# Cross attention and a GELU feed-forward block on one Trainium2 core: batch 1's second product in Strassen form, weight sums on GpSimd, another order of loads and outputs

## The chip, the cores and the metric

The kernel runs on one core of one Trainium2 chip. The metric is the device time of one execution in microseconds. The time before is the median of 8 runs. Beside it there is one profiled execution, whose span runs from its first to its last instruction.

## The reference

Eight batches of eight heads hold 512 rows of x and 32 rows of state, each of 64 columns. Attention goes both ways: every row of x reads the state, and every row of the state reads x. The results stand one below the other (512 + 32 = 544 rows for each batch), the heads side by side (512 columns). These 4352 rows then go through two matrix products with an exact GELU between them.

```python
scores  = scale * x @ state.T          # per batch and head
xread   = softmax(scores)  @ state     # 512 x 64
sread   = softmax(scale * state @ x.T) @ x   # 32 x 64
t = concatenate([xread, sread], rows)  # heads side by side: 4352 x 512
out = gelu(t @ w_in) @ w_out           # w_in 512 x 2048, w_out 2048 x 512
```

Inputs and outputs are float32; the products run on bfloat16 operands.

## The kernel before

The order of the work is written out by hand: a manual schedule, in which every engine executes its instructions in the order of the program text. The 512 rows of x of a batch are worked off batch by batch, and the 32 state rows of all eight batches are collected and go through the two products together at the end.

**Names of the steps.** For batch b:

- `load_x(b)` loads x into one of two buffers (xb) over the GpSimd queue. `rearr` and `rearr_ones` copy it into two layouts (x4, xo), two copies each on GpSimd from batch 2 on. `xtr_dma` transposes x4 by a DMA from SyncE's queue into xT; batch 1 is transposed on TensorE (`xtr`).
- `scores(b, half)` makes the scores on TensorE and their exponentials on ScalarE (e). `norm(b, half)` makes the row sums (cs, L344), their inverses (ics) and the product a = e * ics (L347) on VectorE. `atr` transposes a on TensorE, `atr_dma` by a DMA, into AT.
- `sread` and `sread_out` make the state rows' read-out (srm); `srt(b)` transposes it on TensorE and copies it on VectorE into XSR (L405).
- The first product is reassociated: P = state @ w_in, per head, in four chunks of 512 columns. `p_mm` computes one chunk in two PSUM tiles, `p_copy` copies the first on ScalarE (L426) and the second on VectorE (L427). `pmat` is one chunk; `burst` and `p_run` are several, all products ahead of all copies.
- `M(m, ...)` is `mm1`: the hidden units 128 m to 128 m + 127 of the rows of x, two matmuls of 512 columns and a GELU on ScalarE into g (L485). m counts on over the batches, 16 for each: M(16) is batch 1's first, M(32) batch 2's.
- `U(u)` is `mm2`: a quarter of the sum for one of four output tiles of a batch (j = 0..3), four matmuls of 512 columns (L504). u counts 16 for each batch. `mm2_m(b, m)` is one hidden block m for all four output tiles. With the last quarter VectorE copies the output tile out of PSUM (osb, L491), and SyncE's queue sends it.
- From batch 2 on, the second product is in Strassen form, with h over two halves of the rows, k over two halves of the hidden units and n over two halves of the output columns. `X(b, name)` is one of seven products, 16 matmuls of 256 columns (L602). `g_sum` makes its left operand on VectorE (gsum, L596); its right one is a quarter of w_out or one of five sums of quarters, made once by `w_sums(0)` to `w_sums(4)`, which are called 3, 4, 6, 1 and 7 (L570). The seven results are combined by copies on ScalarE (L640, L648, L652), sums on VectorE (L645, L656, L624, L658) and two instructions on GpSimd (L650, L621).
- `mm1_sr(m)` and `mm2_sr(s)` do the same two products for the state rows (L519, L531), with an output copy (L539) and transfer (L540).

**Order.** Loads stand on the GpSimd queue: w_in and w_out in pieces, then st (state), x(2) and x(3). `load_rest` issues those that are not needed at once. After a prologue for batch 0, the text mixes the steps of batches 0 and 1 by hand up to a first loop (p = 2 to 7), which ends batch 1's M and begins its U. A second loop runs over b = 2 to 7 with eight slots p: each slot has a pair M(16 b + 2 p, + 1) and, for b above 2, one X of the batch before, and in the last two slots X 3 and X 6 of its own. For b = 2 the remaining U of batch 1 stand in that place. In the last batch the slots p = 4 to 7 also take four `mm1_sr` each.

**PSUM.** `ftile` rotates through four banks (ps_f) for most small products. `otile` gives one of four other banks, by turn or by number: 3, 0, 1, 2 for batch 0's four output tiles, j = 0 to 3, and for `p_run(b, (0, 1), ((0, 1), (3, 2)))` banks 0, 1, 3 and 2.

Where POOL, PE, DVE, ACT and SP stand below, these are the profile's names of GpSimd, TensorE, VectorE, ScalarE and SyncE.

Of the kernel before, what the change touches and what calls it, by code (L numbers as in the profile page):

```python
# [10 lines left out]
BF16 = mybir.dt.bfloat16  # L11
# [6 lines left out]
def kernel(  # L18
# [8 lines left out]
    nc = tc.nc  # L27
# [4 lines left out]
    SB = S + NS  # L32
# [34 lines left out]
    w_out_bf = persist.tile([128, MC, d_model], BF16, name="w_out_bf")  # L67
    ident = persist.tile([128, 128], BF16, name="ident")
    sbd = persist.tile([128, B, HC, 2 * NS], BF16, name="sbd")
    XSR = persist.tile([128, HC, B * NS], BF16, name="XSR")  # L70
    g_sr = persist.tile([128, MC, B * NS], BF16, name="g_sr")
    st_f = persist.tile([128, 2, D], FP32, name="st_f")
    st_bf = persist.tile([128, B, 2, D], BF16, name="st_bf")
# [29 lines left out]
    def load_w_in(f0, f1):  # L103
        for t in range(2):
            nc.gpsimd.dma_start(  # L105
                out=w_in_bf[64 * t:64 * t + 64, :, f0:f1],
                in_=moe_w_in[256 * t:256 * t + 256, f0:f1].rearrange("(c d) f -> d c f", c=HC),
            )
# [3 lines left out]
    def load_w_out(i):  # L112
        nc.gpsimd.dma_start(out=w_out_bf[:, 4 * i:4 * i + 4, :], in_=w_out_r[:, 4 * i:4 * i + 4, :])

    def load_x(b):
        xb = xin.tile([128, H, SJ * D], BF16, name="xb", tag="xb")
        nc.gpsimd.dma_start(out=xb, in_=xr[b])
        xbs[b] = xb
# [12 lines left out]


    def load_rest():
        load_w_out(1)
        for f in range(2, FC):
            load_w_in(512 * f, 512 * f + 512)
            load_w_out(f)
        load_st(2, B)
        load_x(2)
        load_x(3)  # L140


# [221 lines left out]
    def atr_dma(b):  # L364
        A = atts[b]
        A.AT = att.tile([128, SJ, 2, 128], BF16, name="AT", tag="AT")
        nc.sync.dma_start_transpose(
            out=A.AT.rearrange("p j t n -> p (j t) n"), in_=A.a
        )
# [29 lines left out]
    def srt(b):  # L399
        A = atts[b]  # L400
        ps = ps_f.tile([128, HC, NS], BF16, name="srT", tag="f")
        nc.tensor.transpose(
            ps.rearrange("p c n -> p (c n)"), A.srm.rearrange("q t d -> q (t d)"), ident
        )
        nc.vector.tensor_copy(out=XSR[:, :, b * NS:(b + 1) * NS], in_=ps)  # L405

    Ps = {}

    def p_mm(b, f, tiles):
        if b not in Ps:  # L410
            Ps[b] = att.tile([128, 2, d_ff], BF16, name="P", tag="P")
        ps = [tiles([128, 512], "p_ps") for t in range(2)]
        for c in range(HC):
            for t in range(2):
                nc.tensor.matmul(  # L415
                    ps[t][32 * c:32 * c + 32, :],
                    lhsT=sbd[64 * t:64 * t + 64, b, c, 32 * t:32 * t + 32],
                    rhs=w_in_bf[64 * t:64 * t + 64, c, f * 512:(f + 1) * 512],
                    start=True,
                    stop=True,  # L420
                )
        return ps

    def p_copy(b, f, ps):
        dst = Ps[b][:, :, f * 512:(f + 1) * 512]
        nc.scalar.copy(out=dst[:, 0, :], in_=ps[0])  # L426
        nc.vector.tensor_copy(out=dst[:, 1, :], in_=ps[1])  # L427

    def pmat(b, f):
        p_copy(b, f, p_mm(b, f, ftile))  # L430

# [82 lines left out]
    def mm1_sr(m):  # L516
        hp = ps_f.tile([128, B * NS], FP32, name="hps", tag="f")
        for c in range(HC):
            nc.tensor.matmul(  # L519
                hp,  # L520
                lhsT=w_in_bf[:, c, m * 128:(m + 1) * 128],
                rhs=XSR[:, c, :],
                start=(c == 0),
                stop=(c == HC - 1),
            )
        nc.scalar.activation(out=g_sr[:, m, :], in_=hp, func=AF.Gelu)

    def mm2_sr(s):
        ps = ps_f.tile([128, d_model], FP32, name="ops", tag="f")
        for m in range(MC):  # L530
            nc.tensor.matmul(  # L531
                ps,
                lhsT=g_sr[:, m, s * 128:(s + 1) * 128],
                rhs=w_out_bf[:, m, :],
                start=(m == 0),
                stop=(m == MC - 1),
            )
        osb = opool.tile([128, d_model], FP32, name="osb", tag="osb")
        nc.vector.tensor_copy(out=osb, in_=ps)  # L539
        nc.sync.dma_start(  # L540
            out=out.rearrange("(b s) n -> b s n", s=SB)[4 * s:4 * s + 4, S:SB, :], in_=osb
        )


    def mm2_m(b, m):
        for j in range(SJ):
            if m == 0:
                ops[b, j] = otile([128, d_model], "op")
            nc.tensor.matmul(  # L549
                ops[b, j],  # L550
                lhsT=gs[b][:, m, j * 128:(j + 1) * 128],
                rhs=w_out_bf[:, m, :],
                start=(m == 0),
                stop=(m == MC - 1),
            )
# [5 lines left out]
    w_sum = {}  # L561

    def w_add(name, x, y, op):
        if name == "3":
            pair = persist.tile([128, 2, MH, NH], BF16, name="ws_34", tag="mix0")
            w_sum["3"], w_sum["4"] = pair[:, 0], pair[:, 1]
        elif name != "4":
            tag = {"6": "mix1", "1": "mix2", "7": "mix3"}[name]
            w_sum[name] = persist.tile([128, MH, NH], BF16, name=f"ws_{name}", tag=tag)
        nc.vector.tensor_tensor(out=w_sum[name], in0=x, in1=y, op=op)  # L570

    def w_sums(i):
        (b11, b12), (b21, b22) = w_q
# [120 lines left out]
    def M(*ms):  # L694
        for m in ms:
            mm1(m // MC, m % MC)

    def U(*us):
        for u in us:
            mm2(u // 16, u % 16 // 4, u % 4)  # L700
# [69 lines left out]
    scores(1, 0)  # L770
    scores(1, 1)
    srt(0)
    U(4, 5)
    rearr_ones(1)
    U(6)
    pmat(0, 2)
    norm(1, 0)
    norm(1, 1)
    U(7)
# [1 line left out]
    sread(1)  # L781
    sread_out(1)
    M(10, 11)
    mm2_m(0, 8)
    mm2_m(0, 9)
    burst([(0, 3), (1, 0)])
    mm2_m(0, 10)
    atr(1)
    M(12, 13)
    srt(1)  # L790
    M(14, 15)
    mm2_m(0, 11)
    begin(2)
    rearr(2)
    xtr_dma(2)
    rearr_ones(2)
    U(12)
    burst([(1, 1), (1, 2)])
    U(13)
    state_prep(2, B)  # L800
    M(16, 17)
    U(14)
    M(18, 19)
    U(15)
    burst([(1, 3), (2, 0), (2, 1)])
    U(16)


    u = 17
    for p in range(2, 8):  # L810
        if p == 4:
            scores(2, 0)
            scores(2, 1)
            norm(2, 0)
            norm(2, 1)
        if p == 7:
            atr_dma(2)
        if p == 3:
            begin(3)
            rearr(3)  # L820
            xtr_dma(3)
            rearr_ones(3)
        M(16 + 2 * p, 17 + 2 * p)
        U(u)
        u += 1
        if p in (5, 7):
            pmat(2, 2 + p // 7)
        if p >= 3:
            w_sums(p - 3)
        if p == 2:  # L830
            nc.gpsimd.tensor_copy(out=hold, in_=gs[1][:, 4, 0:1])
            load_x(4)

    for b in range(2, B):
        nb = b + 1
        for p in range(8):
            k = 16 * b + 2 * p
            if p == 1 and nb < B:
                scores(nb, 0)
                scores(nb, 1)  # L840
            if p in (2, 3) and nb < B:
                norm(nb, p - 2)
            if p == 3 and nb + 1 < B:
                xtr_dma(nb + 1)
            if p == 5 and nb < B:
                atr_dma(nb)
            M(k, k + 1)
            if nb == B and p >= 4:
                for m in range(4 * p - 16, 4 * p - 12):
                    mm1_sr(m)  # L850
            if b == 2:
                for _ in range(2 if p < 4 else 1):
                    if u < 32:
                        U(u)
                        u += 1
            elif p < 5:
                if p == 0:
                    g_sum(b - 1, "5")
                X(b - 1, "45127"[p])
                if p < 3:  # L860
                    g_sum(b - 1, "127"[p])
            if p == 1:
                sread(b)
                sread_out(b)
            if p == 0 and b + 3 < B:
                nc.gpsimd.tensor_copy(out=hold, in_=gs[b][:, 0, 0:1])
                load_x(b + 3)
            if p == 0 and nb + 1 < B:
                begin(nb + 1)
                rearr(nb + 1)  # L870
            if p == 2 and nb + 1 < B:
                rearr_ones(nb + 1)
            if p == 3:
                srt(b)
            if p == 5:
                g_sum(b, "6")
                if nb < B:
                    p_run(nb, (0, 1), ((0, 1), (3, 2)))
            if p == 6:
                X(b, "3")  # L880
            if p == 7:
                if nb < B:
                    p_run(nb, (2, 3), ((1, 2), None))
                X(b, "6")
# [46 lines left out]
```

## Time and profile before

| | us |
|---|---|
| median of 8 runs | 216.72 (215.59 to 218.07) |
| the profiled execution | 217.85 |
| its span | 216.1 |
| PE busy | 202.7 (94%) |
| PEld (weight loads) busy | 129.8 (60%) |
| DVE busy | 128.5 (59%) |
| ACT busy | 131.4 (61%) |
| POOL busy | 65.1 (30%) |

Busy times are unions over the instructions of an engine. PE and PEld are two rows of the same engine, matmuls and weight loads. Matmuls are pipelined, and the length of one in the profile (379 ns for 512 columns) holds its latency; what a stream of them takes is read from the chain of waits, where four take 0.86 us. The chain follows the work that ended last back to its beginning. In the rows of groups the columns are: line, engine, operation, output<-inputs, shapes, count | busy us, mean ns of one | idle us before, and what ended it. A granted clock of 1.00 is TensorE's full speed.

### The profile page before, as it was taken

How to read it: one execution, taken by the hardware profiler on the slowest of the kernel's cores; microseconds unless marked ns; L12 is line 12 of the kernel's file. 1: busy time of each engine (PE TensorE's matmuls, PEld its weight loads, DVE VectorE, ACT ScalarE, POOL GpSimd, SP SyncE). 2: the span in 40 equal slices, each digit the busy share in tenths (PEclk: the TensorE clock that was granted, in tenths of full speed). 3: DMA queues.
4: the chain of work that ended last, by engine and by line, in shares of the span. 5: the costliest groups of instructions: out<-in, count | busy, mean ns of one | idle time of the engine just before them, and what ended most of it. 6: DMA issues, size and time to landing. Idle time of an engine off the chain costs nothing.

```text
span 216.1 us, 4598 instructions
## 1 busy us (share of the span) xinstructions
PE 202.7 (94%) x1929; PEld 129.8 (60%) x1939; DVE 128.5 (59%) x206; ACT 131.4 (61%) x237; POOL 65.1 (30%) x71
## 2 busy tenths in 40 slices
PE   8889999998999999999999999999999969999960
PEld 7535444443444677667765777677667747886740
DVE  2934474739648559965996587558755512026340
ACT  3854865679875877587758775877584534650200
POOL 8954303481360055305571056002200220000400
PEclk9999999999999999999999999999999987999995
DMA  6999999789177619091909500700070010200332
GB/s 204 166 176 204 206 193 177 186 156 175 23 100 177 162 16 176 7 246 13 174 11 293 50 3 2 243 3 2 23 223 3 0 68 34 95 0 3 94 115 85
DMA packets 37837, 23.14 MB, mean 107 GB/s; under 512 B 21688, under 2 KB 35256, under 8 KB 37816
## 3 DMA queue, kind: packets, MB, share of 16 engines
q0 software_dynamic: 13936, 8.10, 27.7%
q1 hardware_dynamic: 23192, 14.29, 27.3%
q10 hardware_dynamic: 688, 0.46, 0.7%
q8 instruction: 15, 0.25, 0.4%
q14 instruction: 6, 0.05, 0.1%
HBM read 17.30 MB, written 8.91 MB: 121 GB/s over the span
## 4 chain that ended last, share of the span: by engine, by line
PE 82%; DMA 6%; POOL 5%; ACT 3%; issue 1%; DVE 0%; POOLq 0%; ACTq 0%
PE xp L602 34%; PE hp L478 24%; PE op L504 9%; DMA w_out_bf<-in_moe_w_out_dram 6%; PE p_ps L415 4%; PE hps L519 4%; PE ops L531 3%; POOL w_in_bf L105 2%; PE op L549 2%; PE pt L324 1%; PE sr L378 1%; POOL sbd L95 1%; ACT g L485 1%; ACT L485 1%; ACT L331 1%
## 5 line engine op out<-in xcount | busy, mean ns | idle before, releaser
L485 ACT ACTIVATE g<-hp 128x512 bf16<-128x512 f32 x124 | 67.5, 603 | 32.5 <-PE hp L478 27.6
L478 PE MATMUL hp<-AT,P 128*128 128x512 bf16 x248 | 63.9, 380 | 0.1
L602 PEld LDWEIGHTS <-gsum 128*128 128x128 bf16 x480 | 46.8, 98 | 12.1 <-issue 2.1
L596 DVE TENSOR_TENSOR gsum<-g 128x2048 bf16<-128x2048 bf16 x30 | 39.8, 1342 | 7.9 <-ACT g L485 6.8
L602 PE MATMUL xp<-ws,gsum 128*128 128x256 bf16 x288 | 34.8, 274 | 0.0
L478 PEld LDWEIGHTS <-P 128*128 128x128 bf16 x248 | 22.3, 98 | 20.4 <-issue 2.9
L427 DVE CAST P<-p_ps 128x512 bf16<-128x512 f32 x31 | 20.0, 684 | 18.5 <-PE p_ps L415 18.5
L650 POOL TENSOR_TENSOR u<-s,oh 128x512 f32<-128x512 f32 x6 | 8.0, 1331 | 71.6 <-ACT oh L648 71.6
L504 PE MATMUL op<-w_out_bf,g 128*128 128x512 bf16 x90 | 23.0, 379 | 0.4 <-DMA w_out_bf<-in_moe_w_out_dram 0.2
L602 PE MATMUL xp<-w_out_bf,gsum 128*128 128x256 bf16 x192 | 22.9, 273 | 0.0
L602 PE MATMUL xp<-ws,g 128*128 128x256 bf16 x192 | 22.9, 273 | 0.0
L426 ACT CAST P<-p_ps 128x512 bf16<-128x512 f32 x31 | 17.0, 604 | 7.6 <-PE p_ps L415 7.6
L602 PEld LDWEIGHTS <-g 128*128 128x128 bf16 x192 | 18.8, 98 | 4.3
L504 PEld LDWEIGHTS <-g 128*128 128x128 bf16 x96 | 9.1, 98 | 11.8 <-issue 1.4
L218 POOL COPY x<-xb 128x1024 bf16<-128x1024 bf16 x12 | 12.6, 1083 | 11.5 <-DMA xb<-in_x_dram 11.5
L228 POOL COPY xo<-xb 128x1024 bf16<-128x1024 bf16 x12 | 14.6, 1242 | 1.3 <-PE sr L378 1.3
L347 DVE TENSOR_TENSOR a<-e,ics 128x512 bf16<-128x512 bf16 x14 | 13.8, 986 | 0.5
L645 DVE TENSOR_TENSOR s<-xp,s 128x512 f32<-128x512 f32 x6 | 4.2, 692 | 14.2 <-PE xp L602 14.2
L621 POOL TENSOR_TENSOR v<-q,oh 128x512 f32<-128x512 f32 x6 | 7.7, 1283 | 13.4 <-ACT oh L652 13.4
L344 DVE TENSOR_REDUCE cs<-e 128x16 f32<-128x512 bf16 x14 | 9.5, 676 | 3.8 <-ACT e L331 3.8
L415 PE MATMUL p_ps<-w_in_bf,sbd 64*32 64x512 bf16 x248 | 10.8, 382 | 0.8 <-ACT g L485 0.7
L519 PE MATMUL hps<-XSR,w_in_bf 128*128 128x256 bf16 x64 | 9.0, 303 | 2.0 <-DVE XSR L405 2.0
(91 smaller groups left out, 196.8 us busy)
## 6 DMA issues: line engine op xcount, KB each, us to landing
out_dram<-oh SPq DMA_DIRECT2D x11, 512.0 KB, 3.3
xb<-in_x_dram POOLq DMA_DIRECT2D x7, 512.0 KB, 7.0
out_dram<-osb SPq DMA_DIRECT2D x9, 256.0 KB, 3.6
w_out_bf<-in_moe_w_out_dram POOLq DMA_DIRECT2D x4, 512.0 KB, 12.5
w_in_bf<-in_moe_w_in_dram POOLq DMA_DIRECT2D x6, 256.0 KB, 12.4
x0f<-in_x_dram SPq DMA_DIRECT2D x3, 256.0 KB, 3.5
w_in_bf<-in_moe_w_in_dram POOLq DMA_DIRECT2D x4, 128.0 KB, 4.2
x0f<-in_x_dram ACTq DMA_DIRECT2D x1, 256.0 KB, 4.3
```

Source lines behind the costliest of these rows:

```text
L218: nc.gpsimd.tensor_copy(out=A.x4[:, :, :, 64 * t:64 * t + 64].rearrange("p j c d -> p c j d"), in_=src[:, t],)
L228: eng.tensor_copy(out=A.xo[:, :, :, 2 + 64 * t:66 + 64 * t].rearrange("p j c d -> p c j d"), in_=src[:, t],)
L347: nc.vector.tensor_tensor(out=A.a[:, :, hs].rearrange("p g (c n) -> p g c n", n=NS), in0=e4, in1=ics[:, :, :].to_broadcast((128, G, 2, NS) ...
L415: nc.tensor.matmul(ps[t][32 * c:32 * c + 32, :], lhsT=sbd[64 * t:64 * t + 64, b, c, 32 * t:32 * t + 32], rhs=w_in_bf[64 * t:64 * t + 64, c ...
L426: nc.scalar.copy(out=dst[:, 0, :], in_=ps[0])
L427: nc.vector.tensor_copy(out=dst[:, 1, :], in_=ps[1])
L478: nc.tensor.matmul(hp, lhsT=Ps[b][:, t, m * 128:(m + 1) * 128], rhs=atts[b].AT[:, :, t, :], start=(t == 0), stop=(t == 1),)
L485: nc.scalar.activation(out=gs[b][:, m, :], in_=hp, func=AF.Gelu)
L504: nc.tensor.matmul(ps, lhsT=gs[b][:, m, j * 128:(j + 1) * 128], rhs=w_out_bf[:, m, :], start=(m == 0), stop=(m == MC - 1),)
L519: nc.tensor.matmul(hp, lhsT=w_in_bf[:, c, m * 128:(m + 1) * 128], rhs=XSR[:, c, :], start=(c == 0), stop=(c == HC - 1),)
L596: nc.vector.tensor_tensor(out=t, in0=g_q(b, h0, k0), in1=g_q(b, h1, k1), op=op)
L602: nc.tensor.matmul(ps[:, j - js[0], :], lhsT=lhs[:, m, 128 * j:128 * j + 128], rhs=rhs[:, m, :], start=(first and j == js[0] and m == 0), ...
```

## The change

- `XSR` gets the order (state row, batch) in its last two dimensions, `mm1_sr` and `mm2_sr` follow it, and the output transfer of `mm2_sr` has 16 outermost rows where it had 4.
- `srt(b)` stands ahead of the pair M in slot p = 3, and no longer at the slot's end.
- `load_rest` loads the third chunk of w_in ahead of the second piece of w_out, and the last piece of w_out after x(2).
- Batch 1's second product takes the Strassen form: its 16 U are gone, and its X stand where those of every other batch stand, X 3 and X 6 ahead of the second loop and the other five in b = 2.
- The steps of batches 0 and 1 stand in another order; the first loop is written out. pmat(0, 2) stands ahead of U(4, 5), with both copies on VectorE. Batch 2's a is transposed on TensorE (`atr`).
- The sums 4, 1 and 7 of `w_sums` go to GpSimd; 3 and 6 stay on VectorE.

```diff
-    XSR = persist.tile([128, HC, B * NS], BF16, name="XSR")
+    XSR = persist.tile([128, HC, NS, B], BF16, name="XSR")
...
     def load_rest():
+        load_w_in(1024, 1536)
         load_w_out(1)
-        for f in range(2, FC):
-            load_w_in(512 * f, 512 * f + 512)
-            load_w_out(f)
+        load_w_in(1536, 2048)
+        load_w_out(2)
         load_st(2, B)
         load_x(2)
+        load_w_out(3)
         load_x(3)
...
-        nc.vector.tensor_copy(out=XSR[:, :, b * NS:(b + 1) * NS], in_=ps)
+        nc.vector.tensor_copy(out=XSR[:, :, :, b], in_=ps)
...
-    def p_copy(b, f, ps):
+    def p_copy(b, f, ps, first=None):
         dst = Ps[b][:, :, f * 512:(f + 1) * 512]
-        nc.scalar.copy(out=dst[:, 0, :], in_=ps[0])
+        (first or nc.scalar.copy)(out=dst[:, 0, :], in_=ps[0])
...
-            out=out.rearrange("(b s) n -> b s n", s=SB)[4 * s:4 * s + 4, S:SB, :], in_=osb
+            out=out.rearrange("(b s) n -> s b n", s=SB)[S + 16 * s:S + 16 * s + 16], in_=osb
...
     def w_add(name, x, y, op):
+        eng = nc.vector if name in "36" else nc.gpsimd
...
-        nc.vector.tensor_tensor(out=w_sum[name], in0=x, in1=y, op=op)
+        eng.tensor_tensor(out=w_sum[name], in0=x, in1=y, op=op)
...
     srt(0)
+    pmat(0, 2, nc.vector.tensor_copy)
     U(4, 5)
     rearr_ones(1)
     U(6)
-    pmat(0, 2)
...
     M(10, 11)
+    burst([(0, 3), (1, 0)])
+    M(12, 13)
+    atr(1)
+    M(14, 15)
     mm2_m(0, 8)
+    srt(1)
     mm2_m(0, 9)
-    burst([(0, 3), (1, 0)])
-    mm2_m(0, 10)
-    atr(1)
-    M(12, 13)
-    srt(1)
-    M(14, 15)
-    mm2_m(0, 11)
+    burst([(1, 1), (1, 2)])
     begin(2)
     rearr(2)
     xtr_dma(2)
     rearr_ones(2)
+    M(16, 17)
+    mm2_m(0, 10)
+    M(18, 19)
+    mm2_m(0, 11)
+    state_prep(2, B)
+    pmat(1, 3)
+    begin(3)
+    rearr(3)
+    xtr_dma(3)
+    rearr_ones(3)
+    M(20, 21)
     U(12)
-    burst([(1, 1), (1, 2)])
+    M(22, 23)
     U(13)
-    state_prep(2, B)
-    M(16, 17)
+    scores(2, 0)
+    scores(2, 1)
+    w_sums(0)
+    w_sums(1)
+    nc.gpsimd.tensor_copy(out=hold, in_=gs[1][:, 4, 0:1])
+    load_x(4)
+    M(24, 25)
     U(14)
-    M(18, 19)
+    norm(2, 0)
+    norm(2, 1)
     U(15)
-    burst([(1, 3), (2, 0), (2, 1)])
-    U(16)
-    u = 17
-    for p in range(2, 8):
...
+    w_sums(2)
+    w_sums(3)
+    w_sums(4)
+    M(26, 27)
+    g_sum(1, "6")
+    p_run(2, (0, 1), ((0, 1), (3, 2)))
+    M(28, 29)
+    X(1, "3")
+    M(30, 31)
+    atr(2)
+    p_run(2, (2, 3), ((1, 2), None))
+    X(1, "6")
...
             if p == 5 and nb < B:
                 atr_dma(nb)
+            if p == 3:
+                srt(b)
             M(k, k + 1)
...
-            if b == 2:
-                for _ in range(2 if p < 4 else 1):
-                    if u < 32:
-                        U(u)
-                        u += 1
-            elif p < 5:
+            if p < 5:
...
-            if p == 3:
-                srt(b)
```

More of the change, by code (lines that the diff above doesn't have):

```diff
@@ L422, in p_mm, with pmat @@
         return ps
-    def p_copy(b, f, ps):
+    def p_copy(b, f, ps, first=None):
         dst = Ps[b][:, :, f * 512:(f + 1) * 512]
-        nc.scalar.copy(out=dst[:, 0, :], in_=ps[0])
+        (first or nc.scalar.copy)(out=dst[:, 0, :], in_=ps[0])
         nc.vector.tensor_copy(out=dst[:, 1, :], in_=ps[1])
-    def pmat(b, f):
-        p_copy(b, f, p_mm(b, f, ftile))
+    def pmat(b, f, first=None):
+        p_copy(b, f, p_mm(b, f, ftile), first)
     def burst(chunks, b_read=None):
@@ L521, in mm1_sr @@
                 lhsT=w_in_bf[:, c, m * 128:(m + 1) * 128],
-                rhs=XSR[:, c, :],
+                rhs=XSR[:, c, :, :].rearrange("p n b -> p (n b)"),
                 start=(c == 0),
@@ L796 @@
     rearr_ones(2)
+    M(16, 17)
[9 more added lines that the diff above has]
+    M(20, 21)
     U(12)
-    burst([(1, 1), (1, 2)])
+    M(22, 23)
     U(13)
-    state_prep(2, B)
-    M(16, 17)
+    scores(2, 0)
[5 more added lines that the diff above has]
+    M(24, 25)
     U(14)
-    M(18, 19)
+    norm(2, 0)
+    norm(2, 1)
     U(15)
-    burst([(1, 3), (2, 0), (2, 1)])
-    U(16)
-    u = 17
-    for p in range(2, 8):
[L811 to L817, printed above, removed]
-        if p == 3:
[L819 to L823, printed above, removed]
-        U(u)
-        u += 1
[L826 to L832, printed above, removed]
+    w_sums(2)
[10 more added lines that the diff above has]
+    X(1, "6")
     for b in range(2, B):
@@ L850 @@
                     mm1_sr(m)
-            if b == 2:
-                for _ in range(2 if p < 4 else 1):
-                    if u < 32:
-                        U(u)
-                        u += 1
-            elif p < 5:
+            if p < 5:
                 if p == 0:
@@ L872 @@
                 rearr_ones(nb + 1)
-            if p == 3:
-                srt(b)
             if p == 5:
```

## The prediction

> **What bounds the kernel now.** I read the chain of waits, then the stages, then single stretches of the timelines. The chain is TensorE nearly from end to end; the stage view (us; PE, PEld, DVE, ACT, POOL busy; granted clock) shows steady batches without any PE idle time and one stage that has some.
>
> ```profile
> PE 82%; DMA 6%; POOL 5%; ACT 3%; issue 1%; DVE 0%; POOLq 0%; ACTq 0%
> 93.25:114.97 21.72, 21.72 (x228) 15.05 (x226) 17.21 (x22) 15.60 (x28) 10.52 (x10) 1.00 0.66 110
> 173.50:179.99 6.49, 4.49 (x25) 2.85 (x23) 0.82 (x2) 2.73 (x6) 1.26 (x1) 0.77 0.20 81
> ```
>
> So a saving must be PE work, a PE wait, or the tail behind the last matmul (span 216.1; the last matmul ends at 209.0). PE waits are few: 2.0 us at 174.7, and about 1.4 us at 48.4 to 51.9, where ACT loads tables for batch 2's exponentials. The first, in the timeline (start, length, instruction, [idle before <- releaser]):
>
> ```profile
> 175.81 0.69 DVE L624 TENSOR_TENSOR oh<-xp,v 128x512 f32<-128x512 f32 x1 [2.79 <-POOL v L621]
> 176.42 0.21 DVE L405 COPY XSR<-srT 128x128 bf16<-128x128 bf16 x1
> 176.69 3.30 PE L519 MATMUL hps<-XSR,w_in_bf 128*128 128x256 bf16 x16 [2.00 <-DVE XSR L405]
> ```
>
> The XSR copy stands on DVE behind L624, which waits for POOL; PE waits for XSR, then runs 16 matmuls in 3.30 instead of 1.75 us at half clock.
>
> A second thing must be seen: DVE instructions with two SBUF inputs stretch while POOL works.
>
> ```profile
> L309 POOL TENSOR_TENSOR a<-e,ics 128x512 bf16<-128x512 bf16 x1 | 1.1, 1117 | 0.0
> L218 POOL COPY x<-xb 128x1024 bf16<-128x1024 bf16 x12 | 12.6, 1083 | 11.5 <-DMA xb<-in_x_dram 11.5
> L570 DVE TENSOR_TENSOR ws<-w_out_bf 128x2048 bf16<-128x2048 bf16 x5 | 6.0, 1217 | 0.0
> 88.68 1.27 POOL L621 TENSOR_TENSOR v<-q,oh 128x512 f32<-128x512 f32 x1 [1.38 <-ACT oh L652]
> 89.30 1.20 DVE L347 TENSOR_TENSOR a<-e,ics 128x512 bf16<-128x512 bf16 x1
> 79.27 2.03 POOL L218 COPY x<-xb 128x1024 bf16<-128x1024 bf16 x2
> 79.87 3.65 DVE L596 TENSOR_TENSOR gsum<-g 128x2048 bf16<-128x2048 bf16 x2
> ```
>
> L347 takes 0.69 undisturbed, here 1.20: POOL's L621 ends at 89.95, L347 0.55 later. The first L596 (1.22 alone) begins inside the POOL pair and streams only after its end at 81.30.
>
> [...] The trace has only 512 columns (1117 ns bf16, 1283 to 1331 fp32)[...] L540's destination has 4 rows outermost; the last two 128 KB transfers behind it land after 5.3 and 4.8 us, 128 KB elsewhere after 2.9. [...] the trace's half-clock stretch after the 2.0 us wait lasts 3.4 us.
>
> **The change, part by part** (lines of before).
>
> *Tail.* srt(7) moves ahead of the matmul pair of p=3, so XSR stands before L624 on DVE: after gsum (ends 173.03), ready at 173.3. PE then needs .06+.87+1.75+.87 from 171.0 and reaches L519 at 174.55, the 16 matmuls end at 176.4 instead of 179.99, and the next product loses its 0.3 slow start: **-3.9**. ACT's copies and Gelus (ends at 175.5) keep ahead. XSR's strided output (8 copies of 216 ns, unmeasured in this form) may double unseen. 16 outermost rows in L540: the last transfers should land some 2.8 us after issue at 209.5, not 4.8: **-2.0** (bounds 0, if it isn't spread, to -2.5).
>
> *PE work.* Batch 1: 64 matmuls of 512 columns at 0.216 (four take 0.86) are 13.8; 112 of 256 at 0.109 (sixteen take 1.75) are 12.2: -1.6. Batch 2's attention transpose goes from DMA to PE: +0.45 (as at 31.76). Products add DVE sums, ACT copies and POOL instructions to b=2, as every later batch has them at 21.7 with no PE idle.
>
> *Loads.* In load_rest two w_in pieces go before w_out(1), which then lands where they landed together with it: 24.63 instead of 22.34. PE fills 0.4 of that with pmat(0,2) and waits: +1.8. Bursts directly ahead of the M that reads their copies or buffers: +0.75 before M(12), +0.55 before M(16); st_ps's buffer before M(21): +0.45. pmat(0,2)'s two copies on DVE (2 x 0.68) delay L228, and with it only the issue of x(3) at about 25, whose turn in the queue comes after 36. Walk: 24.63 + 18.9 of PE work (eight M pairs, six U, four mm2_m at 0.865 are 15.6; small steps 2.7; 0.1 at each change of kind) + 1.75 waits = 45.2, scores of batch 2; they are now followed by U work, so the 1.4 us ACT wait is gone. Four M, two U and the scores later PE stands at p_run(2,(0,1)) at **49.4**.
>
> *Weight sums.* Sums 4, 1 and 7 go to POOL: 2048 columns at 1117/512 ns would be 4.5[...], without its fixed share of the short row 4.1; I take 4.3 (at the copy's rate, the lower bound, 2.1). POOL is in order: x(3) lands at 38.7 to 40 (38.66 before; the same bytes stand ahead of it, and the transpose of x(2) now runs beside it), rearr(3) and rearr_ones(3) 4.05 (as at 36.05), so sum 4 starts near 43.3. DVE wants sum 3 at 46.0, after osb of U(13)[...]. From here:
> - sum 4 ends 47.6, sum 3 (DVE) 48.8;
> - hold and the issue of x(4), 0.85 (57.95 to 58.80): sum 1 from 49.65 to 53.95. DVE meanwhile does osb U(14), cs and ics, and asks for L347 at 50.4, 0.7 too late: it runs at 54.5;
> - [...] the second L347 ends at 59.4. If POOL's sums follow each other without a gap, as the L218 pair did, the end is 1.0 later;
> - osb of U(15) stands behind that L347 on DVE: 60.0, or 61.0.
>
> p_run's fourth tile lies in U(15)'s PSUM bank (4,5,7,6 against 7,4,5,6 for j=0..3), so PE stands until **60.6**, the middle of the two and some 0.1 of handing over. That wait swallows the early ones. What follows on PE before M(32): rest of p_run 0.35, M 0.97, X3 1.75, M 0.87, atr 0.45, p_run 0.56, X6 1.85 = 6.8; DVE's queue (sum 6, gsum, four P copies, 5 us) is done before X6. Half clock after 11 idle us costs 1.7 to 3.4; I take 2.2. M(32) at 69.6, M(48) 21.7 later at 91.3, against 76.45 before: **+14.85**.
>
> *Queues.* SP: x(3)'s transpose now stands before batch 0's four outputs; osb has 4 buffers, nobody waits. AT(2)'s DMA is gone from it.
>
> Sum: 14.85 - 3.9 - 2.0 = **+8.95**. Span 216.1 becomes 225.0; the profiled execution took 217.85, 1.75 around its span, and stands 1.13 above the median 216.72, within the runs (215.59 to 218.07). Applied to the median: **225.7**.
>
> **Rivals.**
>
> *A, above (0.65).* 222 to 229.5 by x(3)'s landing, 4.1 to 4.5 per sum, clock and tail.
>
> *B, one sum less in front (0.16).* If L347 is asked for before POOL takes sum 1 (margin 0.7 us)[...], only one more sum delays osb U(15): PE goes on 4.6 us sooner, **221.1** (217.5 to 222). For it: the margins. [...]
>
> *C, faster: the sums on POOL are short (0.15).* At the copy's 2.1 us, or if long POOL instructions let DVE in between, osb U(15) comes with PE. Then PE passes at 49.7, M(32) at 56.1, M(48) 77.8: +1.3; with the tail -4.6: **212.1**. It decides from about 2.25 us per sum: PE goes on at 43.3 + 3 x 2.25 + 3.8 (the rest of the list above) = 53.85, without the cold clock M(48) at 53.85 + 6.8 + 21.7 = 82.35, 5.9 late, as much as the tail gains. Against it: the two-input row of 1117 ns for 512 columns, twice the copy's rate.
>
> *D, part of the change does nothing.* If the output isn't spread, or XSR is late through another wait, 2.0 or 3.9 are missing: up to 229.6 with A; over the range 0.04.
>
> **How the numbers follow.** The likeliest case gives 225.7, its own range 222 to 229.5. To hold 8 in 10 the range takes in B: **217 to 229.5**; C and the end of D stay out. Within 0.5% (1.1 us, about what a measurement of this kernel tells from no change) lie the edges of B and C, 0.03; faster 0.16, slower 0.81.
>
> **What would show it.** In the profile after: three POOL TENSOR_TENSOR on ws near 4.3 us each; DVE's L347 of batch 2 stretched to 4 us and more; a PE idle stretch of about 11 us before p_ps near 50, released by osb on DVE, then a granted clock of 0.5; L519 without idle time before it; the last two transfers landing within 3 us. POOL sums of 2.25 us or less, or no PE gap near 50, make the prediction wrong, and then the time lies below 217.

## The result, and the profile after

The changed kernel takes **226.43 us** (median of 11 runs, 225.42 to 228.28), against 216.63 for the kernel before beside it (32 runs, 215.22 to 218.09): ratio **1.046 [1.043, 1.049]**, slower by 9.8 us. Forecast were 225.7 us and a range of 217 to 229.5. The profiled execution of after took 228.68 around a span of 226.9. It is one of the slower ones, 2.25 above its median; the lines below come from it, so its difference to the profile of before, 226.9 - 216.1 = 10.8, is 1.0 larger than that of the medians.

The chain of waits of after comes first. Before, it named PE with 82% and DVE with 0%.

```profile
PE 61%; DVE 22%; DMA 11%; issue 2%; POOL 1%; ACT 1%; SPq 0%; DVEq 0%; POOLq 0%
```

More than a fifth of the span now runs through DVE. Where that is, the stage view tells (stretch; length, then PE, PEld, DVE, ACT, POOL busy; granted clock; DMA share; GB/s):

```profile
49.00:63.00 14.00, 4.14 (x27) 1.30 (x26) 13.86 (x11) 5.29 (x9) 7.15 (x2) 0.74 0.44 88
92.80:114.99 22.19, 21.98 (x228) 15.03 (x225) 17.67 (x23) 15.65 (x27) 8.11 (x8) 1.00 0.49 107
186.00:193.00 7.00, 7.00 (x76) 5.11 (x61) 3.13 (x6) 4.02 (x8) 1.96 (x2) 1.00 0.01 2
```

In the 14 us from 49 on PE works 4.14 and DVE is "busy" for 13.86. A steady batch (second row) takes 22.19, where it took 21.72. In the last batch (third row) PE no longer stands still. PE's timeline has the waits of the first stretch:

```profile
50.84 0.39 PE L416 MATMUL p_ps<-w_in_bf,sbd 64*32 64x512 bf16 x1
57.90 0.63 PE L416 MATMUL p_ps<-w_in_bf,sbd 64*32 64x512 bf16 x8 [6.67 <-DVE osb L492]
61.71 0.62 PE L416 MATMUL p_ps<-w_in_bf,sbd 64*32 64x512 bf16 x7 [3.19 <-DVE osb L492]
```

Both are p_run(2, (0, 1)), which waits for a PSUM bank, first for osb of U(14), then for osb of U(15). What DVE did meanwhile, in its timeline:

```profile
47.03 0.69 DVE L492 COPY osb<-op 128x512 f32<-128x512 f32 x1 [1.04 <-PE op L505]
47.64 9.60 DVE L572 TENSOR_TENSOR ws<-w_out_bf 128x2048 bf16<-128x2048 bf16 x1
57.16 0.68 DVE L492 COPY osb<-op 128x512 f32<-128x512 f32 x1
57.77 0.67 DVE L345 TENSOR_REDUCE cs<-e 128x16 f32<-128x512 bf16 x1
...
58.76 0.69 DVE L348 TENSOR_TENSOR a<-e,ics 128x512 bf16<-128x512 bf16 x1
...
60.37 0.69 DVE L348 TENSOR_TENSOR a<-e,ics 128x512 bf16<-128x512 bf16 x1
60.97 0.69 DVE L492 COPY osb<-op 128x512 f32<-128x512 f32 x1
61.57 1.22 DVE L572 TENSOR_TENSOR ws<-w_out_bf 128x2048 bf16<-128x2048 bf16 x1
```

And POOL's:

```profile
43.01 4.06 POOL L572 TENSOR_TENSOR ws<-w_out_bf 128x2048 bf16<-128x2048 bf16 x1
47.02 0.18 POOL L816 COPY hold<-g 128x1 bf16<-128x1 bf16 x1
47.15 0.92 POOL L117 DMA_DIRECT2D xb<-in_x_dram  x1
48.08 8.07 POOL L572 TENSOR_TENSOR ws<-w_out_bf 128x2048 bf16<-128x2048 bf16 x2
```

Read the two side by side. Sum 3 on DVE, the same instruction as the one of 1.22 us at 61.57, is shown from 47.64 for 9.60 us. POOL's sums 1 and 7 end at 56.15, sum 3 about 1.1 later: one instruction, held up by two of POOL's. Behind it, in order, stand osb of U(14), the norms of batch 2, and osb of U(15), which PE waits for.

The end of after, in the timelines of DVE and PE: the copy into XSR and the first matmuls that read it. In before 2.00 us of idle time and half clock (granted 0.55 from 176.69 to 180.00) stood there.

```profile
190.67 0.72 DVE L406 COPY XSR<-srT 128x128 bf16<-128x128 bf16 x1
192.26 1.91 PE L520 MATMUL hps<-XSR,w_in_bf 128*128 128x256 bf16 x16
```

And the last two transfers in the list of DMA issues (KB each, us from issue to landing), first of after:

```profile
out_dram<-oh SPq DMA_DIRECT2D x1, 128.0 KB, 2.6
out_dram<-oh ACTq DMA_DIRECT2D x1, 128.0 KB, 2.2
```

The same two transfers of before:

```profile
out_dram<-oh SPq DMA_DIRECT2D x1, 128.0 KB, 5.3
out_dram<-oh ACTq DMA_DIRECT2D x1, 128.0 KB, 4.8
```

They land in about half the time; behind the last matmul (ends 222.88) the span of after goes on for 4.0 us, in before 7.1.

### The profile page after: what moved, and what is told of

Same layout as the page of the kernel before. It is cut to its first block, busy times and chain, and to the rows that moved or that the text cites. A ratio compares the mean times of both kernels' runs of the same rounds, so it can differ in the third digit from the quotient of the medians.

```text
span 226.9 us, 4723 instructions
## 1 busy us (share of the span) xinstructions
PE 206.7 (91%) x1989; PEld 136.2 (60%) x1995; DVE 146.2 (64%) x211; ACT 132.9 (59%) x239; POOL 79.2 (35%) x76
## 4 chain that ended last, share of the span: by engine, by line
PE 61%; DVE 22%; DMA 11%; issue 2%; POOL 1%; ACT 1%; SPq 0%; DVEq 0%; POOLq 0%
PE xp L604 28%; PE hp L479 17%; DVE gsum L598 7%; DMA w_out_bf<-in_moe_w_out_dram 5%; DVE ws L572 4%; PE p_ps L416 4%; DVE a L348 3%; PE hps L520 3%; PE op L505 3%; PE ops L532 3%; DMA AT<-a 3%; DMA x0f<-in_x_dram 3%; DVE cs L345 2%; PE op L550 1%; DVE ics L347 1%
## 5 line engine op out<-in xcount | busy, mean ns | idle before, releaser
L604 PEld LDWEIGHTS <-gsum 128*128 128x128 bf16 x560 | 54.3, 98 | 13.9 <-issue 2.3
L598 DVE TENSOR_TENSOR gsum<-g 128x2048 bf16<-128x2048 bf16 x35 | 46.8, 1354 | 7.9 <-ACT g L486 6.8
L604 PE MATMUL xp<-ws,gsum 128*128 128x256 bf16 x336 | 40.2, 273 | 0.0
L604 PE MATMUL xp<-ws,g 128*128 128x256 bf16 x224 | 27.8, 279 | 0.0
L604 PE MATMUL xp<-w_out_bf,gsum 128*128 128x256 bf16 x224 | 26.7, 273 | 0.0
L604 PEld LDWEIGHTS <-g 128*128 128x128 bf16 x224 | 22.5, 100 | 5.9 <-issue 0.5
L416 PE MATMUL p_ps<-w_in_bf,sbd 64*32 64x512 bf16 x248 | 13.1, 396 | 10.4 <-DVE osb L492 9.9
L348 DVE TENSOR_TENSOR a<-e,ics 128x512 bf16<-128x512 bf16 x14 | 15.1, 1080 | 0.5
L416 PEld LDWEIGHTS <-sbd 64*32 64x32 bf16 x248 | 3.1, 89 | 20.1 <-issue 19.8
L572 POOL TENSOR_TENSOR ws<-w_out_bf 128x2048 bf16<-128x2048 bf16 x3 | 12.1, 4058 | 0.0
L572 DVE TENSOR_TENSOR ws<-w_out_bf 128x2048 bf16<-128x2048 bf16 x2 | 10.8, 5408 | 0.0
```

The lines of the kernel that those rows point to most:

```text
L348: nc.vector.tensor_tensor(out=A.a[:, :, hs].rearrange("p g (c n) -> p g c n", n=NS), in0=e4, in1=ics[:, :, :].to_broadcast((128, G, 2, NS) ...
L416: nc.tensor.matmul(ps[t][32 * c:32 * c + 32, :], lhsT=sbd[64 * t:64 * t + 64, b, c, 32 * t:32 * t + 32], rhs=w_in_bf[64 * t:64 * t + 64, c ...
L572: eng.tensor_tensor(out=w_sum[name], in0=x, in1=y, op=op)
L598: nc.vector.tensor_tensor(out=t, in0=g_q(b, h0, k0), in1=g_q(b, h1, k1), op=op)
L604: nc.tensor.matmul(ps[:, j - js[0], :], lhsT=lhs[:, m, 128 * j:128 * j + 128], rhs=rhs[:, m, :], start=(first and j == js[0] and m == 0), ...
```

## The experiments

My theory after the result: the sums on POOL cost some 7 us through the instruction that they block on DVE (sum 3, 9.60 us for 1.22) and through what stands behind it; the new loads about 2; the tail gives 4 to 6, less something for the strided copy. Rivals: the new order of the text alone brings PE to the PSUM wait; or the sums' length alone is to blame. Ratios are those to the kernel before, measured beside each kernel, with a 95% interval. They need not equal the quotient of the two medians: for tail_srt the medians lie 3.1 us apart, and the ratio gives 3.9 (2.7 to 5.1).

| kernel | median us | ratio |
|---|---|---|
| after | 226.43 | 1.046 [1.043, 1.049] |
| sums_dve | 219.38 | 1.011 [1.008, 1.014] |
| sums_copy | 220.5 | 1.011 [1.004, 1.018] |
| dve_order | 223.83 | 1.033 [1.029, 1.037] |
| loads | 219.62 | 1.011 [1.008, 1.014] |
| tail_srt | 213.84 | 0.982 [0.976, 0.988] |
| tail_out | 216.92 | 0.997 [0.994, 1.000] |
| tail_both | 212.6 | 0.982 [0.978, 0.987] |
| best_tail | 216.65 | 1.001 [0.998, 1.003] |
| tail_rhs | 237.29 | 1.098 [1.093, 1.104] |
| tail_pool | 211.23 | 0.975 [0.970, 0.980] |
| strassen_dve | 216.66 | 1.000 [0.998, 1.002] |
| strassen_pool | 210.48 | 0.973 [0.968, 0.978] |

**sums_dve: after, with all five sums on DVE.**

```diff
-        eng = nc.vector if name in "36" else nc.gpsimd
+        eng = nc.vector
```

> The changed kernel with all five weight sums on VectorE, in the same places of the text. [...] sum 3 takes 1.2 us instead of 9.6, sum 4 follows it, osb of U(15) ends near 54.6 instead of 61.7, and TensorE's wait at the P tiles falls from about 10 to about 3.5 us; some of it comes back where the P copies stand behind sums 6, 1, 7 and gsum on VectorE (about 1.6), and 0 to 2 us of half clock go: 219 to 221 us. If the new order of the steps and the added Strassen work on VectorE cause the wait (theory of the order), 3.6 us more of sums on VectorE make it no better: 226 us or more.

Measured 219.38: 7.0 us less than after by the medians and 7.6 by the ratios, with the order of the text, loads and tail unchanged. So the sums on POOL, not the order, make most of the loss. DVE takes all five sums in 5.83 us (2.35 for two, 3.48 for three), less than the 9.60 of the one that was blocked in after. 219.38 is still above before: part of the loss lies elsewhere. PE's timeline has it:

```profile
52.41 0.41 PE L416 MATMUL p_ps<-w_in_bf,sbd 64*32 64x512 bf16 x7 [3.01 <-DVE osb L492]
```

This is the same wait for osb of U(15), which stands behind the norms of batch 2 on DVE whoever makes the sums.

**sums_copy: after, with POOL's three additions replaced by copies of their first operand** (the sums 4, 1 and 7 are left out, so this kernel does less).

```diff
-        eng.tensor_tensor(out=w_sum[name], in0=x, in1=y, op=op)
+        if name in "36":
+            nc.vector.tensor_tensor(out=w_sum[name], in0=x, in1=y, op=op)
+        else:
+            nc.gpsimd.tensor_copy(out=w_sum[name], in_=x)
```

> The changed kernel with GpSimd's three two-input sums replaced by copies of their first operand (the additions of sums 4, 1 and 7 are left out). A copy of 2048 columns should take 2.1 us where the sum took 4.06. [...] GpSimd's second and third end near 50.4 instead of 56.2, VectorE's sum 3 shrinks from 9.6 to about 4, osb of U(15) ends near 55.8 instead of 61.7: 5.8 us less, 0 to 2 us of half clock less: 218.5 to 220.6 us. The prediction's break-even of 2.25 us per sum would say 216 to 217. Theory of the order: 226 us, sum 3 unchanged.

Measured 220.5, as the theory had it. POOL's timeline, then DVE's:

```profile
45.06 0.87 POOL L117 DMA_DIRECT2D xb<-in_x_dram  x1
45.92 3.73 POOL L574 COPY ws<-w_out_bf 128x2048 bf16<-128x2048 bf16 x2
```

```profile
45.16 5.58 DVE L572 TENSOR_TENSOR ws<-w_out_bf 128x2048 bf16<-128x2048 bf16 x1
```

A copy takes 1.90 us, less than half of a sum. DVE's sum 3 waits again through two POOL instructions in a row, 45.92 to 49.65. It was there at 45.16, before the first of them, while POOL issued x(4); the last section comes back to that. At 1.90 us per instruction the prediction's rival C has this kernel faster than before; that is refuted here, since the waits for osb remain (2.65 and 3.40 us).

**dve_order: after, with the norms of batch 2 and sum 3 behind U(15) and its osb; sums on POOL as in after.**

```diff
-    w_sums(0)
...
+    U(15)
+    w_sums(0)
...
-    U(15)
```

> The changed kernel with GpSimd's sums where they were, but VectorE's sum 3 and the two norms of batch 2 behind U(15) and its output copy. [...] the output copies no longer stand behind sum 3: no wait at p_run(2,(0,1)); TensorE stops at X 3 instead, for sum 3 at about 57.3, and at p_run(2,(2,3)) for the P copies. 222 us. [...]

Measured 223.83: 2.6 below after. With both osb ahead of sum 3, PE no longer waits for them, but the wait comes back one step on, for the sum itself, as PE's and then DVE's timeline show:

```profile
57.06 1.25 PE L604 MATMUL xp<-ws,g 128*128 128x256 bf16 x5 [6.85 <-DVE ws L572]
```

```profile
48.10 8.90 DVE L572 TENSOR_TENSOR ws<-w_out_bf 128x2048 bf16<-128x2048 bf16 x1
```

POOL's pair of sums runs here from 47.83 to 55.90. DVE's sum 3 came 0.27 us after the pair had begun and ended 1.1 us after it; between the two sums it did not get in. The place of the blocked instruction decides who waits; that it is blocked costs most of the time in every place.

**loads: before, with the changed load order and pmat(0, 2) moved ahead of U(4, 5), both its copies on VectorE.**

```diff
     def load_rest():
+        load_w_in(1024, 1536)
         load_w_out(1)
...
+    pmat(0, 2, nc.vector.tensor_copy)
     U(4, 5)
```

> The kernel before with the changed order of loads and pmat(0,2) ahead of U(4,5) with both copies on VectorE, and nothing else. w_out(1) lands near 24.3 to 24.6 instead of 22.3, TensorE waits 1.1 to 1.3 us ahead of U(4); the prediction's +1.8 us, 218.7 us. Rival: the freed ScalarE and the earlier third chunk win it back later: 216.9 us.

Measured 219.62, by the ratio +1.1% or 2.4 us. U(4) waits for w_out(1), in PE's timeline:

```profile
23.70 3.61 PE L505 MATMUL op<-w_out_bf,g 128*128 128x512 bf16 x16 [1.35 <-DMA w_out_bf<-in_moe_w_out_dram]
```

The rest isn't in this trace: the profiled execution took 217.78 at a mean granted clock of 0.991, and the runs spread from 217.44 to 222.45. The four longest, from 221.47 on, have a mean clock of 0.975. An estimate from these clocks: 0.025 of their span of 220 us is 5.5 us lost, against 1.9 in the profiled execution, so if all clock that is lost is lost time, it accounts for about 3.6 of the 3.7 to 4.7 us between them. Where in the kernel it fell isn't recorded; in after's profile a stretch of half clock, 25.1 to 28.5 (granted 0.50), follows the same wait. The load order and the moved pmat were not taken apart.

**tail_srt: before, with srt(b) ahead of M in slot p = 3.**

```diff
+            if p == 3:
+                srt(b)
             M(k, k + 1)
...
-            if p == 3:
-                srt(b)
```

> The kernel before with srt(b) ahead of the pair M in slot p = 3 and nothing else. The prediction: 3.9 us less, 212.7 us, no idle time ahead of the first L519. Rival: the earlier transpose takes a PSUM buffer of the rotation one step sooner and holds it until VectorE's copy, which costs each batch about 0.4 us as in the changed kernel (22.2 against 21.7 us per batch): 2 us of the gain come back, 214.5 us.

Measured 213.84, by the ratio -1.8% or 3.9 us. No idle time is left before L519, whose first matmuls start at 174.41 (forecast 174.55), and the last matmul of the kernel ends at 205.0 rather than 209.0.

**tail_out: before, with XSR in the order state row, batch, and 16 outermost rows.** (The lines of the change that name XSR and the output transfer; srt stays where it was.)

> The kernel before with XSR in the order state row, batch, and 16 outermost rows in the state rows' output transfer, srt(b) where it was. The end behind the last matmul falls from 7.1 us to about 4, as in the changed kernel: 213.5 us. If the strided copy into XSR (0.72 us in the changed kernel instead of 0.22) is what costs 0.4 us per batch, it shows here too (per batch 22.1 us): 215.5 us.

Measured 216.92, -0.3%. The last two transfers land 2.6 and 2.2 us after issue, and the end behind the last matmul shrinks from 7.1 to 4.5 us. Yet most of it is gone: DVE's copy into XSR takes 0.71 to 0.73 us rather than 0.22, and PE waits 2.50 us for it at the end, where it waited 2.00. In two batches in between PE also waits 0.27 and 0.32 us for L658, which stands behind that copy on DVE.

**tail_both: before, with both** (the whole tail of after).

> The whole tail of the changed kernel on the kernel before: transpose of the read-out (srt) ahead of the matmuls of p=3 in every batch, XSR in the order state row, batch, 16 outermost rows in the output transfer; no Strassen form for batch 1, loads and sums as before. If the parts add up: before 216.7, the earlier srt -3.9 (as measured alone), the end behind the last matmul 4.5 rather than 7.1 (-2.6), the strided copy into XSR 0.72 us on VectorE in each batch +1.8 (batches of 22.1 to 22.2 rather than 21.7): 212.0. Rival: the strided copy stands ahead of more on VectorE once it is in front of the pair of p=3, and each batch loses 0.5 and more: 213.5 or above.

Measured 212.6, near the 212.0 of the sum. PE's timeline shows part of the price, in two batches:

```profile
90.96 0.59 PE L478 MATMUL hp<-AT,P 128*128 128x512 bf16 x2 [0.17 <-DVE XSR L405]
113.15 0.59 PE L478 MATMUL hp<-AT,P 128*128 128x512 bf16 x2 [0.21 <-DVE XSR L405]
```

M waits for a PSUM bank that the copy into XSR empties.

**best_tail: before, with srt ahead in the last batch alone, XSR contiguous as in before, and ScalarE's GELU of `mm1_sr` writing the new order.**

```diff
-        nc.scalar.activation(out=g_sr[:, m, :], in_=hp, func=AF.Gelu)
+        nc.scalar.activation(
+            out=g_sr[:, m, :].rearrange("p (n b) -> p b n", b=B),
+            in_=hp.rearrange("p (b n) -> p b n", b=B),
+            func=AF.Gelu,
+        )
```

> The kernel before with the two gains of the tail and without their cost: srt stands ahead of M in slot p = 3 in the last batch alone, XSR stays in the order batch, state row, and ScalarE's Gelu of mm1_sr writes its result in the order state row, batch, so that the output transfer has 16 outermost rows. 216.9 - 4.0 (tail_srt, by its span) - 2.6 (tail_out: 4.5 instead of 7.1 us behind the last matmul) = 210.3 us. If the permuted write makes the Gelu (388 ns) so slow that TensorE waits for it, 212 us or more.

Measured 216.65: nothing gained, so the worse of the two expectations. The group of these GELUs, here and then in before:

```profile
L526 ACT ACTIVATE g_sr<-hps 128x256 bf16<-128x256 f32 x16 | 19.2, 1633 | 0.0
```

```profile
L526 ACT ACTIVATE g_sr<-hps 128x256 bf16<-128x256 f32 x16 | 5.9, 388 | 3.7 <-PE hps L519 3.4
```

The same 256 columns take 1.2 us of ACT's time each (19.2 / 16), not 0.37, and PE waits for them in nearly every step from 180 to 192. From the last read-out to the last matmul the kernel takes 42.6 us, where tail_srt takes 37.1.

**tail_rhs: the same, but TensorE reads XSR in the new order, and ScalarE writes as in before.**

```diff
-                rhs=XSR[:, c, :],
+                rhs=XSR[:, c, :].rearrange("p (b n) -> p n b", b=B),
```

> Kernel before, with srt ahead of p=3 in the last batch alone, XSR contiguous as in before, 16 outermost rows in the output transfer, and the order state row, batch made by TensorE's moving operand: mm1_sr reads XSR with a stride of 64 bytes between neighbours (256 columns, 64 matmuls). ScalarE's Gelu writes contiguously (it took 1.2 us per tile where it wrote with a stride of 16 bytes, and TensorE waited 0.54 us and more for it). If TensorE reads the strided operand at its usual pace: 216.7 - 3.9 - 2.6 = 210.2. Rival: the strided read halves TensorE's pace, 64 matmuls at 0.218 rather than 0.109: +7, about 217.

Measured 237.29, far above both. The timeline of PE, where 16 matmuls of 256 columns take 1.91 when they read contiguously:

```profile
180.82 3.10 PE L602 MATMUL xp<-ws,gsum 128*128 128x256 bf16 x16
184.62 7.04 PE L519 MATMUL hps<-XSR,w_in_bf 128*128 128x256 bf16 x16
```

With 64 bytes between neighbours of its moving operand a matmul takes four times as long here: 0.43 us (184.62 to 191.48, where the next row starts, over 16), not 0.109. The clock falls too: the row above it, an ordinary one, takes 3.10, at a granted clock of 0.68 (180.8 to 184.6). The order made in the stationary operand of `mm2_sr` instead (tail_lhs) gave no time, so that way stays open.

**tail_pool: the new order made by POOL.** DVE copies contiguously into a buffer XB; POOL rewrites it into XSR; only the last batch is written with the stride by DVE. As in best_tail, srt stands ahead in the last batch alone.

```diff
+        if b == B - 1:
+            nc.vector.tensor_copy(out=XSR[:, :, :, b], in_=ps)
+        else:
+            nc.vector.tensor_copy(out=XB[:, :, b, :], in_=ps)
+            nc.gpsimd.tensor_copy(out=XSR[:, :, :, b], in_=XB[:, :, b, :])
```

> Kernel before, with srt ahead of the matmuls of p=3 in the last batch alone, 16 outermost rows in the output transfer and XSR in the order state row, batch, but VectorE keeps its short contiguous copy of 0.22 us: for batches 0 to 6 it writes a buffer XB, and POOL, which has time, rewrites it with the stride into XSR; only the last batch is written with the stride by VectorE (0.72 us, where TensorE did not wait for it in tail_both). If the 0.72 us copies on VectorE were what lengthened the batches: batches of 21.7 as in before, and 216.4 - 3.9 - 2.6 = 209.9. Rival: POOL's strided copies[...] delay VectorE's instructions or POOL's own L621, and the batches stay at 22.1: 211.9, about tail_both (212.6).

Measured 211.23, -2.5%: faster than before and after. From one read-out to the next (82.36 to 104.02) a batch takes 21.66 us again, where tail_both takes 22.14 and tail_out 22.09, so the strided copy on DVE was what lengthened this batch. POOL's copy takes as long, but nobody waits for it. The batch behind it still takes 22.58, with the wait of the second line:

```profile
91.43 0.76 POOL L410 COPY XSR<-XB 128x128 bf16<-128x128 bf16 x1 [1.34 <-DVE XB L409]
120.81 1.04 PE L483 MATMUL hp<-AT,P 128*128 128x512 bf16 x4 [0.69 <-DMA AT<-a]
```

The second line, from PE's timeline, is part of the 1.3 that is missing to the 209.9 expected: one batch waits for the DMA transpose of a. It isn't explained here; tail_both (0.38) and tail_srt (0.26) have it too, so it doesn't come from POOL's copies alone. Against tail_both the gain isn't settled: the intervals overlap, the place of srt differs as well, and the two profiled spans differ by 0.2 us only.

**strassen_dve: best_tail with batch 1 in Strassen form**, all sums on DVE (two of them near 35 us), osb ahead of the norms, before's loads.

> Batch 1 in Strassen form, all sums on VectorE, sums 3 and 6 near 35 us while GpSimd and VectorE are idle, output copies ahead of the norms, loads in the order of before, tail as in best_tail. TensorE's work is 1.15 us less than best_tail's, and its 1.4 us wait for ScalarE's tables at 48 to 52 goes; some new waits for VectorE of 0.5 to 1.5 us: 208.5 to 209.5 us. If Strassen's additions on VectorE cost more than they save, 210.5 us or more.

Measured 216.66, the same as best_tail: the saving isn't to be seen, and a new wait of 1.01 us for w_in stands at 30.03, in a burst ahead of which two products of batch 0 stood in before. They had been moved behind that burst. The slow GELUs of best_tail are in it as well.

**strassen_pool: that kernel with tail_pool's tail, and three products of batch 0 moved back.**

```diff
-    burst([(0, 3), (1, 0)])
     mm2_m(0, 8)
+    mm2_m(0, 9)
+    burst([(0, 3), (1, 0)])
+    mm2_m(0, 10)
...
-    mm2_m(0, 9)
...
-    mm2_m(0, 10)
```

> As tail_pool, with the Strassen form for batch 1 (six weight sums on VectorE, two of them near 35 us, loads as before, osb ahead of the norms of batch 2), and with one product of batch 0 moved back ahead of the burst that waited 1.01 us for w_in in strassen_dve. PE work -1.6 for the Strassen form, +0.45 for atr(2) on TensorE; what it waits for ACT near 50 us was 1.45 in strassen_dve and 1.4 in before. If nothing else is late: 1.1 below tail_pool, about 208.8. Rival: another wait takes the saving, as in strassen_dve against best_tail (216.66 and 216.65): within 0.4 of tail_pool.

Measured 210.48, -2.7%, the lowest median of all, 0.75 below tail_pool; the intervals overlap, so the last step isn't settled by the times. In the traces the read-out of batch 2 starts at 60.13 rather than 61.84. Of these 1.7 us, 0.9 are there at the first read-out (19.67 and 20.57), ahead of the first step in which the two kernels differ; the 0.8 left are less than the 1.15 expected. The wait for w_in is gone, and no wait for the transpose follows. The wait for ACT near 50 us stays:

```profile
48.68 1.91 PE L608 MATMUL xp<-ws,g 128*128 128x256 bf16 x16 [0.86 <-ACT P L431]
```

**Where the 9.8 us are,** an estimate: the sums on POOL 226.43 - 219.38 = +7.0; the loads +2.4 and the tail -3.8 (ratios of loads and tail_both). The remainder, 9.8 - 7.0 - 2.4 + 3.8 = +4.2 (with ratios throughout 3.8), is the new order of batches 0 to 2 with Strassen's -1.2 in it. Of that, the wait of 3.01 us above is seen, and half clock follows it (mean 0.72 from 52 to 58 us in sums_dve, 1.7 us lost); it rests on the parts adding up, which they need not do, and was not taken alone. The same Strassen form with osb ahead of the norms and the sums early (strassen_pool) has no such wait.

## Why the prediction was right, and which of its steps were not

The forecast of 225.7 stands 0.7 below the median, and the case is A.

- **The mechanism: right.** POOL's sums hold DVE (sum 3 takes 9.60 us, not 1.22), osb of U(15) is late, and PE stands before the fourth tile of p_run. sums_dve shows it: without POOL's sums 7 us less. The size is right in part by luck, as the items below tell.
- **Which instruction is blocked: wrong.** The prediction let sum 3 run at 47.6, and the norms' product (L347 of before, L348 of after) was to be the blocked one, twice. The step that failed is "sum 4 ends 47.6, sum 3 (DVE) 48.8", a turn for DVE between two of POOL's instructions. In the profile U(13) was later than the walk said, and sum 3 came at 47.64, not at 46.0. Sum 4 was over by then and POOL issued x(4); yet sum 3 ran only when sums 1 and 7 had ended at 56.15. The norms then took 0.69 each.
- **The end of the wait: near by luck, two errors that largely cancel.** POOL was done at 56.15, not at 58.8 (54.5 + 4.3): sums of 4.06 us rather than 4.3 (0.7 of it), and no turn for DVE between them. But 5.5 us of DVE work stood behind POOL's end (rest of sum 3, norms, both osb), not 1.2 to 2.2. PE went on at 61.71, not 60.6.
- **M(48) at +16.35 (92.80), not +14.85:** 1.1 from this, and 0.44 from the batch before it, 22.14 us rather than 21.7. From PE's going on to M(32) it was 8.95 us; the sum had 6.8 + 2.2 = 9.0.
- **The half clock** lasted from 55.8 to 66.1 (granted 0.50), and cost the 2.2 us assumed, which were an estimate (half of the 3.4 us stretch in before is 1.7): from 61.7 on PE works at half clock for 4.4 us, which fits the item above. How long a wait must be to bring it on is not shown: in before half clock (0.55 from 176.69 to 180.00) follows a wait of 2.00 us, and in after (0.50 from 25.1 to 28.5) one of 1.12.
- **The loads:** w_out(1) landed at 24.64 for 24.63 forecast; PE stood 0.43 + 1.12 for 1.8 forecast. PE reached p_run 1.4 later than forecast. Whether the later wait swallowed this is not settled. No wait of PE delays POOL's sums (sum 4 starts at 43.01, right behind the copies of x(3), forecast 43.3); but sum 3 came 1.6 later than forecast, and one that came during sum 4 might have got its turn. In before's order the same loads cost 2.4.
- **srt earlier: -3.9, right** (tail_srt: 3.9 by its ratio, 4.0 from last matmul to last matmul in the traces). "XSR's strided output may double unseen" was wrong twice. It takes 0.72 rather than 0.22, and though unseen at L520, it is seen in the batches: 22.19, 22.19 and 21.81 from read-out to read-out, where before had 21.66, 21.71 and 21.44, 1.4 us together. From M(48) to the last matmul after is therefore 2.5 us shorter than before, not 3.9. With XSR's step of 16 bytes the copy takes 3.3 times as long (0.72 for 0.22), and with one of 64 bytes TensorE's matmul takes 4 times as long (0.43 for 0.109, tail_rhs); what about a step costs this, no run shows.
- **16 outermost rows: -3.1, not -2.0.** From issue to landing 2.6 and 2.2 us rather than 5.3 and 4.8, which is 2.6 to 2.7, and the bound of -2.5 was too tight; tail_out, with this alone, had 2.6. The transfers spread over more engines: near their end the mean busy share of the 16 DMA engines was 0.24 in before (212 to 214, 84 GB/s) and 0.83 in after (223 to 225, 256 GB/s). The other 0.5 of after lies behind the last landing: from there to the end it is 1.8 us in before and tail_out, 1.3 in after and in strassen_pool. What takes it stays open.
- **Rival C's break-even of 2.25 us per sum: refuted.** sums_copy is below it with 1.90 and still slower than before, by 1.1% [0.4, 1.8]. Even with no sum on POOL the kernel is slower by 1.1%. The term that was too small is the 3.8 in "43.3 + 3 x 2.25 + 3.8": PE goes on at 55.21 in sums_copy, which is 43.1 + 3 x 1.90 + 6.4, and at 61.71 in after, which is 43.0 + 3 x 4.06 + 6.5. It left out the DVE work that POOL's sums pile up, and that the norms stand ahead of osb in any case. Nor do the rival's own figures agree: by that sum, instructions of 2.1 us let PE go on at 53.4, not at its 49.7, so its 212.1 doesn't follow from them.

## What to carry to other kernels

A side engine with idle time is not a free engine: work moved to POOL is priced by what it does to DVE's queue, so look at which two-input DVE instruction will be waiting then (in after, osb's copy out of PSUM took its usual 0.69 us at 45.30, inside POOL's sum 4, and sum 3, with both inputs in SBUF, 9.60), at everything in order behind it, and at who waits for that; here 12.1 us of POOL took the place of 3.5 us of DVE and cost some 7. If a layout is changed for the sake of a transfer, ask which engine will write or read with the stride, and give that to one for which nobody waits; the same reordering gained some 2 us (tail_pool against tail_srt, with overlapping intervals) or cost over 20 (tail_rhs), according to the engine. Put copies that empty PSUM ahead of anything on the same queue that can be held up (dve_order: 2.6 us below after).

## What the runs showed that I had not expected

POOL held DVE's sum over two instructions in a row, but did not hold every DVE instruction so long. DVE's sum 3 was held for 9.60, 8.90 and 5.58 us, each time through two of POOL's, though in after and in sums_copy it was there before the first of them. Later in after, L348 waits for the first of two POOL copies only (DVE's timeline, then POOL's):

```profile
101.29 1.53 DVE L348 TENSOR_TENSOR a<-e,ics 128x512 bf16<-128x512 bf16 x1
101.24 2.49 POOL L229 COPY xo<-xb 128x1024 bf16<-128x1024 bf16 x2
```

The first copy ends at 102.27 and L348 at 102.82, inside POOL's pair, and the pair takes 2.49 us instead of the 2.03 it takes from 41.01. What decides between the two cases, these traces don't tell. That POOL was issuing x(4) when sum 3 came (from 47.15 for 0.92 us in after, from 45.06 for 0.87 in sums_copy) doesn't alone explain the early hold: in strassen_pool a sum on DVE starts during such an issue and takes its 1.22 us.

```profile
43.98 1.22 DVE L576 TENSOR_TENSOR ws<-w_out_bf 128x2048 bf16<-128x2048 bf16 x1
43.37 0.87 POOL L118 DMA_DIRECT2D xb<-in_x_dram  x1
```

What differs in after and sums_copy is that POOL's next sums follow the issue without a gap; that this is the reason was not tested.

Two sets of prices:

- A two-input sum of 2048 bf16 columns takes 4.06 us on POOL (one of 512 columns 1.12, L309 in before) and 1.16 to 1.22 on DVE; a copy of 2048 on POOL 1.90.
- One element at a time with a step of 16 bytes: 0.72 us for DVE's 128 columns instead of 0.22, 0.76 on POOL, 1.2 instead of 0.37 for ScalarE's 256. TensorE with a step of 64 bytes: 0.43 instead of 0.109 for 256 columns.
